# Retention and two gated layers on one core: pairs adjacent in memory, a decay table spread by a product, a mask made on the chip, work moved between engines, and rewritten order tables

## The chip, the cores and the metric

The kernel runs on one core of a Trainium2 chip. The metric is the device time of one execution in microseconds (us), median over runs. A core has TensorE (PE in the rows; PEld is its loading of weights), VectorE (DVE), ScalarE (ACT), GpSimd (POOL) and SyncE (SP, which only issues transfers here); 16 DMA engines move data between the chip's main memory and SBUF. PE writes to the eight banks of PSUM; DVE and ACT read and write PSUM and SBUF, and here POOL works on SBUF alone.

## What is computed

```python
gamma = 1.0 - 2.0 ** (-5.0 - np.arange(H))            # H = 8 heads, D = 64
for t in range(S):                                     # S = 768, batch 2
    state = gamma * state + outer(k[:, :, t], v[:, :, t])
    y[:, :, t] = (1 / sqrt(D)) * q[:, :, t] @ state
x = y.transpose(0, 2, 1, 3).reshape(1536, 512)
x = ((x @ w_a) * (x @ w_b)) @ w_out                    # d_ff 1536, first layer
h = x @ w_in                                           # d_ff 2048, second layer
out = (h * sigmoid(1.702 * h)) @ w_out2
```

q, k and v are float32; the five weight matrices arrive as 8-byte floats.

## The kernel before, in words

**Retention.** The 1536 tokens are 12 blocks of 128, six to a sequence (`SEQ`). For block n PE makes scores (`att_scores`, the "sc" products into `ps_sc`), adds the block's keys and values to a running state (`att_kv`, into `ps_kv`, which ACT copies to one of two `state` tiles), and makes the output from the masked scores (first half of `att_av`) and, but for a sequence's first block, from the state (second half, line 255), both into `ps_av`, of which there are three. Around it DVE multiplies the scores by the mask `causal` into `a` (line 207); `q` is multiplied by a decay table `qdec` and `v` by `vdec`, on POOL (lines 178 and 186, both recorded at helper line 75). Of `qdec`, `[P, SEQ, NP, P]`, one block's part is loaded and ACT makes the other five from it by a scale per partition (line 169). The four inputs of a block lie in memory as q, k transposed, k, v; the tile `qv` takes the first and the last, `kk` the two in between. Four buffers of each are there.

**Strassen sums and two parts.** The layers use products of halves (seven instead of eight, numbered 1 to 7 in `Job.step`), and each operand as a high part (a cast to float32r, on ACT) and a low part (source minus high part, `lo_part`, line 66), with three matmuls for each product. The rows of the first layer come from the retention: for each pair of blocks DVE forms sums (`att_x_vector`) and the tiles `a1h/a1l`, `s12h/s12l`, `s34h/s34l` and `a22` (shown as `a`). An `att_x_vector` chain and the low part of `s12` must be done before the block's `ps_av` bank can be written again.

**Weights.** A unit of weights is loaded into `wraw`, turned into float32 by ACT (`w_carry`) and DVE (`w_bits`, `w_sign`, `w_add`), summed (`w_sums`, four operations into `tt`) and split: `wd` for products 1 to 3, `wt` for the others (`w_hi` on ACT, `w_lo` on DVE). Units 0 to 11 are the first layer's jobs, 18 to 25 the second's.

**Order.** Each engine runs its instructions in the order in which the program emits them. In the retention the order inside a block is written out in the loop, with `BLOCK` telling which step of unit 0 or 1 goes where. `up` goes through products in the order `HEAD`, a loop, `TAIL`; after each, the table `UP` says how many steps of the weight stream (w) and of the postponed row work (l) are emitted. `down` does the same with `DOWN`, in "quarters" q of the output. A product 2 follows product 1 in the same PSUM pair `x`; products 6, 5, 3 follow each other in the pair `y`, into which ACT has copied `x` (line 722), and between them ACT copies `y` out (u2 after 6 at line 728, u4 after 5 at line 730). So product 3 cannot begin before the copy of u4 has read `y`. The very last quarter is done column group by column group:

```python
if last and q == 3:
    a = new_set("x")
    banks = [a[:, 0], a[:, 1], new_set("d")]
    for n in range(NG):
        for f in block:
            product(q, f, (n,), banks)
        flush(q, [(banks[n], n * G, (n + 1) * G)])
```

Before the first scores, and between the first blocks, PE runs 27 matmuls on zeros (`warm`).

Of the kernel before, what the change touches and what calls it, by code (L numbers as in the profile page):

```python
# [40 lines left out]
def retention_moe_kernel(  # L41
# [68 lines left out]

    causal = attp.tile([P, 1, P], F32, tag="causal", name="causal", bufs=1)
# [8 lines left out]
    qv_t, kk_t, q_t, v_t, a_t, x_t = {}, {}, {}, {}, {}, {}  # L120
# [3 lines left out]
    def att_load(n, part):  # L124
        if n >= NBLK:
            return
        if part == "qv":
            qv_t[n] = qv = attp.tile([P, 2, DM], F32, tag="qv", name="qv", bufs=RAWBUFS)
            if n > 0:
                nc.sync.dma_start(out=qv, in_=att[n][:, 0:4:3, :])  # L130
        else:
            kk_t[n] = kk = attp.tile([P, 2, DM], F32, tag="kk", name="kk", bufs=RAWBUFS)
            if n > 0:

                m = 1 if n % SEQ == SEQ - 1 else 2
                nc.sync.dma_start(out=kk[:, 0:m, :], in_=att[n][:, 1:1 + m, :])
        if n == 0 and part == "kk":
            qv = qv_t[n]
            nc.sync.dma_start(out=qv[:, 0, :], in_=att[n][:, 0, :])
            nc.scalar.dma_start(out=kk[:, 0, :], in_=att[n][:, 1, :])  # L140
            nc.scalar.dma_start(out=causal[:, 0, :], in_=cmask[:, 0:P])
            nc.scalar.dma_start(
                out=vdec[:, 0].rearrange("p h o -> p (h o)"), in_=cdec[:, NP * P:NP * P + H]
            )
            nc.sync.dma_start(out=qv[:, 1, :], in_=att[n][:, 3, :])
            nc.sync.dma_start(out=kk[:, 1, :], in_=att[n][:, 2, :])
            nc.scalar.dma_start(out=qdec[:, 1].rearrange("p a t -> p (a t)"), in_=cdec[:, 0:NP * P])
# [25 lines left out]
    def att_q(n):  # L173
        if n < NBLK:
            t = attp.tile([P, NP, P], F32, tag="q", name="q", bufs=3)
            q = qv_t[n][:, 0, :].rearrange("p (a t) -> p a t", t=P)
            for k in (slice(0, NP),) if n == 1 else (slice(0, 2), slice(2, NP)):
                mul(nc.vector if n == 1 else nc.gpsimd, t[:, k], q[:, k], qdec[:, n % SEQ, k])
            q_t[n] = t

    def att_v(n):
        if n < NBLK:
            t = attp.tile([P, H, D], F32, tag="v", name="v", bufs=3)
            v = qv_t[n][:, 1, :].rearrange("p (h d) -> p h d", d=D)
            for k in (slice(0, NP), slice(NP, H)):
                mul(nc.gpsimd, t[:, k], v[:, k], vdec[:, n % SEQ, k].to_broadcast([P, NP, D]))
            v_t[n] = t

    def att_scores(n):
# [4 lines left out]
        q = qv_t[n][:, 0, :].rearrange("p (a t) -> p a t", t=P) if n == 0 else q_t[n]  # L194
        for p in range(NP):
            for h2 in range(2):
# [3 lines left out]
                    kk_t[n][rows, 0, p * P:(p + 1) * P],  # L200
# [14 lines left out]
    def att_kv(n):  # L215
# [7 lines left out]
        for p in range(NP):  # L223
            for h2 in range(2):
# [3 lines left out]
                    kk_t[n][:, 1, h * D:(h + 1) * D],  # L228
# [108 lines left out]
    def att_s_lo(n):  # L337
        if n > 0 and n % 2 == 1:
            hi, lo = s_parts(n, 0)
            lo_part(nc.vector, lo, halves(av_t.pop(n)), hi)  # L340
            t, right = x_t.pop(n - 1), x_t.pop(n)
# [5 lines left out]
            later.append(lambda: [lo_part(nc.vector, lo, src, hi) for (hi, lo), src in parts])  # L347
# [17 lines left out]
    units = [*units_of(1), *units_of(2)]  # L365
    wraw, wt, wtt = {}, {}, {}
# [114 lines left out]
    def d_operand(f, part):  # L481
# [6 lines left out]
        (0, 1): (('load', 0),),  # L488
        (1, 0): (('load', 1),),
        (1, 1): (('load', 2),),  # L490
        (2, 2): (('load', 3),),
        (3, 1): (('load', 0),),
        (4, 1): (('carry', 0), ('bits', 0)),
        (5, 0): (('sign', 0),),
        (6, 0): (('d', 0), ('load', 1)),
        (7, 1): (('add', 0), ('later', 0)),
        (8, 1): (('load', 2),),
        (9, 0): (('load', 3),),
        (9, 2): (('carry', 1),),
        (10, 0): (('later', 0), ('bits', 1)),  # L500
        (11, 2): (('load', None), ('sums', 0)),
# [3 lines left out]
        (1, 2): ('', 'lll'),  # L505
        (1, 3): ('', 'ww'),
# [590 lines left out]
```

## Time and profile before

| | us |
|---|---|
| median of 3 runs | 589.77 (589.14 to 589.82) |
| the profiled execution's own time | 590.43 |
| its span in the trace | 588.60 |
| PE busy in the span | 572.1 |
| retention ends, first product of the first layer starts | 55.8 |
| DVE busy in the span | 418.8 |

Times in the trace count from the start of the span; 1.83 us of the profiled execution's own time lie around it. PE is busy for 97% of the span, but busy is not the same as needed: the warm-up matmuls count too, and a stretch with waits is found only when PE's idle time is read stage by stage.

### The profile page before, as it was taken

Reading aid. Unit: us, or ns where it says so; the run is one execution under the profiler, and the core shown is the slowest. Engines: PE = TensorE matmul, PEld = TensorE weight load, DVE = VectorE, ACT = ScalarE, POOL = GpSimd, SP = SyncE. Lnnn points to the kernel's source line nnn. Section 1 sums busy time; section 2 is a strip of 40 time slices with the busy share of each in tenths; the row PEclk is TensorE's granted clock in tenths of the full one; section 3 lists DMA queues with packets and bytes.
Section 4 is the critical chain, followed back from the end, with each engine's and each line's share of the span. In section 5 each row is a group of like instructions: output and inputs, shape, how many; then the busy total and the mean of one; then the engine's idle time right before and its main releaser. Section 6 shows DMA issues by size and latency. Waiting matters only on the chain.

```text
span 588.6 us, 8444 instructions
## 1 busy us (share of the span) xinstructions
PE 572.1 (97%) x3448; PEld 523.9 (89%) x3448; DVE 418.8 (71%) x478; ACT 296.2 (50%) x366; POOL 69.2 (12%) x145
## 2 busy tenths in 40 slices
PE   8978999999999999999999999999999999999996
PEld 8877999999999999888888889999998888888885
DVE  3789989788969788925788798766668636677322
ACT  3676654456545446535243578666667745160100
POOL 7783002021212111200000000000000000000000
PEclk9999999999999999999999999999999999999999
DMA  8992224433342221533422013665521635340022
GB/s 298 352 340 75 72 71 179 134 137 124 105 146 72 72 84 60 232 126 107 144 69 74 1 45 129 217 218 180 178 81 64 232 126 185 119 161 1 0 109 107
DMA packets 24583, 76.90 MB, mean 131 GB/s; under 512 B 2400, under 2 KB 2528, under 8 KB 24544
## 3 DMA queue, kind: packets, MB, share of 16 engines
q1 hardware_dynamic: 23968, 75.77, 37.2%
q10 hardware_dynamic: 576, 0.59, 0.4%
q8 instruction: 27, 0.44, 0.3%
q14 instruction: 12, 0.10, 0.1%
HBM read 60.62 MB, written 15.73 MB: 130 GB/s over the span
## 4 chain that ended last, share of the span: by engine, by line
PE 85%; DVE 9%; DMA 3%; ACT 1%; issue 1%; POOL 0%; ACTq 0%; DVEq 0%
PE ps L679 45%; PE ps L923 38%; DMA kk<-in_att_dram 2%; DVE a L207 1%; DVE s12l L66 1%; DVE sum L69 1%; DMA causal<-in_cmask_dram 1%; DVE sum L72 1%; DVE s34l L66 1%; PE ps_sc L198 1%; DVE a L66 1%; DVE x L69 1%; PE ps_av L244 0%; DVE wt L433 0%; DVE wt L66 0%
## 5 line engine op out<-in xcount | busy, mean ns | idle before, releaser
L923 PE MATMUL ps<-wt,ghl 128*128 128x512 f32 x576 | 131.1, 389 | 0.8 <-DVE sum L72 0.8
L923 PEld LDWEIGHTS ps<-wt,ghl 128*128 128x128 f32 x576 | 108.0, 188 | 23.6 <-DVE sum L72 1.2
L923 PE MATMUL ps<-ghl,wt 128*128 128x512 f32 x432 | 98.1, 389 | 0.0
L923 PEld LDWEIGHTS ps<-ghl,wt 128*128 128x128 f32 x432 | 81.1, 188 | 16.8
L679 PE MATMUL ps<-s12h,wt 128*128 128x384 f32 x320 | 87.2, 335 | 1.4 <-ACT ps L722 0.9
L679 PE MATMUL ps<-a1h,wd 128*128 128x384 f32 x320 | 87.4, 335 | 0.7 <-ACT ps L722 0.7
L66 DVE TENSOR_TENSOR ghl<-g,ghl 128x1536 fp32r<-128x1536 f32 x28 | 49.5, 1767 | 47.5 <-ACT ghl L272 47.5
L272 ACT CAST ghl<-g 128x1536 fp32r<-128x1536 f32 x28 | 40.9, 1482 | 56.2 <-PE ps L923 41.4
L72 DVE TENSOR_TENSOR sum<-ps,sum 128x512 f32<-128x512 f32 (+1 forms) x41 | 36.9, 932 | 39.0 <-PE ps L923 39.0
L679 PEld LDWEIGHTS ps<-s12h,wt 128*128 128x128 f32 x320 | 58.2, 188 | 2.1 <-ACT ps L722 1.2
L679 PEld LDWEIGHTS ps<-a1h,wd 128*128 128x128 f32 x320 | 58.3, 188 | 1.4 <-ACT ps L722 1.0
L679 PE MATMUL ps<-s12l,wt 128*128 128x384 f32 x160 | 53.7, 336 | 0.4 <-DVE s12l L66 0.3
L679 PE MATMUL ps<-a1l,wd 128*128 128x384 f32 x160 | 53.5, 334 | 0.0
L75 POOL TENSOR_TENSOR g<-g,u 128x768 f32<-128x768 f32 x12 | 30.0, 2500 | 162.5 <-DVE u L72 111.6
L433 DVE CUSTOM_DVE_ANT_0 wt<-wraw,wt 128x2048 uint16<-128x2048 uint16 x34 | 45.4, 1334 | 2.0
L679 PE MATMUL ps<-s34h,wd 128*128 128x384 f32 x160 | 44.2, 336 | 2.7 <-ACT u L730 2.7
L72 DVE TENSOR_TENSOR u<-ps,u 128x768 f32<-128x768 f32 x28 | 26.8, 955 | 27.3 <-PE ps L679 25.8
L679 PE MATMUL ps<-a,wt 128*128 128x384 f32 x240 | 44.8, 334 | 0.0
L679 PE MATMUL ps<-s34h,wt 128*128 128x384 f32 x160 | 43.8, 334 | 0.0
L679 PEld LDWEIGHTS ps<-a,wt 128*128 128x128 f32 x240 | 41.9, 188 | 0.0
L427 DVE SCALAR_TENSOR_TENSOR wt<-wraw,wt 128x1024 int32<-128x1024 int32 x34 | 41.4, 1218 | 0.4
L414 ACT ACTIVATE wt<-wraw 128x1024 f32<-128x1024 f32 x34 | 38.9, 1145 | 2.7 <-DMA kk<-in_att_dram 2.7
(92 smaller groups left out, 811.1 us busy)
## 6 DMA issues: line engine op xcount, KB each, us to landing
wraw<-in_w_dram SPq DMA_DIRECT2D x64, 512.0 KB, 4.5
spilled<-g SPq DMA_DIRECT2D x16, 768.0 KB, 7.4
g<-spilled SPq DMA_DIRECT2D x16, 768.0 KB, 6.0
qv<-in_att_dram SPq DMA_DIRECT2D x11, 512.0 KB, 7.1
kk<-in_att_dram SPq DMA_DIRECT2D x9, 512.0 KB, 7.1
wraw<-in_w_dram SPq DMA_DIRECT2D x8, 256.0 KB, 7.5
out_dram<-sum SPq DMA_DIRECT2D x3, 512.0 KB, 2.8
out_dram<-sum SPq DMA_DIRECT2D x6, 256.0 KB, 2.4
```

What stands on the lines that cost most here:

```text
L66: engine.tensor_tensor(out=lo, in0=src, in1=hi.bitcast(F32), op=ALU.subtract)
L69: nc.vector.tensor_tensor(out=o, in0=a, in1=b, op=ALU.subtract)
L72: nc.vector.tensor_tensor(out=o, in0=a, in1=b, op=ALU.add)
L75: engine.tensor_tensor(out=o, in0=a, in1=b, op=ALU.mult)
L198: nc.tensor.matmul(ps[:, h2, p * P:(p + 1) * P], kk_t[n][rows, 0, p * P:(p + 1) * P], q[rows, p, :], start=(p == 0), stop=True, skip_group ...
L207: nc.vector.tensor_tensor(out=a, in0=ps.rearrange("p c (a t) -> p (c a) t", t=P), in1=causal.to_broadcast([P, 2 * NP, P]), op=ALU.mult,)
L272: nc.scalar.copy(hi, src)
L414: nc.scalar.activation(out=wt[i], in_=high.bitcast(F32), func=ACTF.Abs)
L427: nc.vector.scalar_tensor_tensor(out=ti, in0=wraw[i][:, :, 1], scalar=-0x40000000, in1=ti, op0=ALU.bitwise_and, op1=ALU.bitwise_or)
L433: nc.vector.tensor_tensor(out=ti, in0=ti, in1=wraw.pop(i)[:, :, 0], op=ALU.add)
L679: nc.tensor.matmul(ps[b][:, 0] if len(ps) > 1 else ps[0][:, b], w_operand(self.key, i, wp)[:, kc * P:(kc + 1) * P], r.operand(i, xp)[:, kc ...
L923: nc.tensor.matmul(banks[n], l, r, start=(f == block[0] and i == 0), stop=(f == block[-1] and i == 2), skip_group_check=True,)
```

## The change

1. A block's inputs are taken as two adjacent pairs, `qk` (q and transposed k) and `vk` (k and v), each with one transfer; all loads go through SP, those of blocks 0 and 1 first. The layout in main memory is as it was.
2. The table of q's decay for one block is no longer loaded (256 KB). Two rows of it are, into a zeroed tile `pair`, and one PE product (`att_qdec_first`) spreads them over 128 partitions; ACT copies the result to `qdec`. Of the constants for its other parts, three of five are made by POOL products instead of memsets.
3. The mask is a memset and an `affine_select` on POOL, in place of a 64 KB load and a DVE comparison.
4. `ELSEWHERE`: ACT scales some heads of v (23 heads in nine blocks); q of blocks 3 and 4 goes to DVE; in the layers POOL makes the sums of seven units, six `wt` and five `wd` low parts (DVE before), and DVE makes six of the twelve gate products that POOL made.
5. `ORDER`, `BLOCK`, `UP`, `DOWN`, `HEAD` and `TAIL` are rewritten. 16 of the 27 warm-up matmuls go.
6. The last quarter of the second layer puts each column group in a PSUM bank of its own.
7. Buffers of the rows are counted free when the low part is emitted and no earlier (`row_done`); `att_s_lo` is cut in two.

The core of the diff:

```diff
+    def att_qdec_first():
+        ps = ps_att.tile([P, NP, P], F32, tag="av", name="ps_qdec", bufs=3).rearrange("p a t -> p (a t)")
+        nc.tensor.matmul(
+            ps, pair[:, NP * P:NP * P + P], pair[:, 0:NP * P], start=True, stop=True, skip_group_check=True
+        )
+        nc.scalar.copy(qdec[:, 1].rearrange("p a t -> p (a t)"), ps)
...
-            for k in (slice(0, NP), slice(NP, H)):
-                mul(nc.gpsimd, t[:, k], v[:, k], vdec[:, n % SEQ, k].to_broadcast([P, NP, D]))
+            heads = H - ELSEWHERE.get(("v", n), 0)
+            for k in (slice(0, NP), slice(NP, heads)) if heads > NP else (slice(0, heads),):
+                mul(nc.gpsimd, t[:, k], v[:, k], vdec[:, n % SEQ, k].to_broadcast([P, k.stop - k.start, D]))
+            for h in range(heads, H):
+                nc.scalar.activation(
+                    out=t[:, h], in_=v[:, h], func=ACTF.Copy, scale=vdec[:, n % SEQ, h]
+                )
...
-        lo_part(nc.gpsimd if key in POOL_LO.get(kind, ()) else nc.vector, t[:, 1, 0:n], src, t[:, 0, 0:n])
+        on_pool = ELSEWHERE.get((kind, units.index(("j", *key))), 0) if len(key) == 3 and key in job_keys else 0
+        lo_part(nc.gpsimd if on_pool else nc.vector, t[:, 1, 0:n], src, t[:, 0, 0:n])
...
     TAIL = {
-        1: ((-1, 7), (0, 1), (-1, 3), (0, 2), (0, 6), (-1, 4), (0, 7), (0, 5), (0, 3), (0, 4)),
-        2: ((0, 1), (-1, 7), (-1, 3), (0, 2), (0, 6), (-1, 4), (0, 5), (0, 7), (0, 3), (0, 4)),
+        1: ((0, 1), (-1, 7), (0, 2), (0, 6), (0, 7), (0, 5), (-1, 3), (-1, 4), (0, 3), (0, 4)),
+        2: ((0, 1), (-1, 7), (0, 2), (0, 6), (-1, 3), (0, 7), (0, 5), (-1, 4), (0, 3), (0, 4)),
     }
...
                 if last and q == 3:
-                    a = new_set("x")
-                    banks = [a[:, 0], a[:, 1], new_set("d")]
+                    banks = [new_set("d") for _ in range(NG)]
```

In `TAIL` an entry is (job, product), job 0 being the stage's last and -1 the one before it. In the first stage, first half of this table, PE's rows show what lies between product 5 and product 3 of the last job; `ps` with its number is the PSUM tile, `s12`, `s34` and `a22` are row operands, `wt` and `wd` weights. Before, the end of product 5 (into `ps_2231`) and the start of product 3 (into the same tile):

```order
702 L679 MATMUL ps_2231<-s12h_428,wt_2094 128x384 x2
703 L679 MATMUL ps_2231<-s12l_429,wt_2094 128x384
704 L679 MATMUL ps_2231<-s12h_428,wt_2094 128x384
705 L679 MATMUL ps_2231<-s34h_451,wd_2072 128x384
706 L679 MATMUL ps_2231<-s34l_452,wd_2072 128x384
707 L679 MATMUL ps_2231<-s34h_451,wd_2072 128x384 x2
```

The same place in the changed program, from the end of product 5 (into `ps_2190`) to the start of product 3:

```order
692 L992 MATMUL ps_2190<-s12h_404,wt_2124 128x384
693 L992 MATMUL ps_2070<-s34h_428,wd_1998 128x384
694 L992 MATMUL ps_2070<-s34l_429,wd_1998 128x384
695 L992 MATMUL ps_2070<-s34h_428,wd_1998 128x384 x2
696 L992 MATMUL ps_2070<-s34l_429,wd_1998 128x384
697 L992 MATMUL ps_2070<-s34h_428,wd_1998 128x384 x2
698 L992 MATMUL ps_2070<-s34l_429,wd_1998 128x384
699 L992 MATMUL ps_2070<-s34h_428,wd_1998 128x384 x2
700 L992 MATMUL ps_2070<-s34l_429,wd_1998 128x384
701 L992 MATMUL ps_2070<-s34h_428,wd_1998 128x384
702 L992 MATMUL ps_2208<-a22_430,wt_2020 128x384 x12
703 L992 MATMUL ps_2190<-s34h_428,wd_2088 128x384
```

Products 3 and 4 of the job before, 24 matmuls into other tiles, now stand between the two.

On PE at the start of the program (`ps_warm` the warm-up, `ps_sc` scores, `ps_kv` keys and values, `ps_av` output), before:

```order
1 L965 MATMUL ps_warm<-state_82 128x128 x11
2 L198 MATMUL ps_sc<-qv,kk 128x128 x8
3 L965 MATMUL ps_warm<-state_82 128x128 x8
4 L226 MATMUL ps_kv<-v,kk 64x64 x8
5 L244 MATMUL ps_av<-a,v 64x128 x8
6 L965 MATMUL ps_warm<-state_82 128x128 x3
7 L198 MATMUL ps_sc<-q,kk 128x128 x8
8 L965 MATMUL ps_warm<-state_82 128x128 x5
9 L198 MATMUL ps_sc<-q,kk 128x128 x8
```

and in the changed program:

```order
1 L1291 MATMUL ps_warm<-state_82 128x128 x11
2 L275 MATMUL ps_sc<-qk 128x128 x8
3 L195 MATMUL ps_qdec<-pair 128x512
4 L303 MATMUL ps_kv<-v,vk 64x64 x8
5 L275 MATMUL ps_sc<-q,qk 128x128 x8
6 L321 MATMUL ps_av<-a,v 64x128 x16
7 L332 MATMUL ps_av<-q,state_83 64x128 x8
8 L303 MATMUL ps_kv<-v,vk 64x64 x8
9 L275 MATMUL ps_sc<-q,qk 128x128 x16
```

The warm-ups after the first scores are gone, the product that spreads the decay table stands third, and the scores of block 2 (now in row 9, before in row 9 too) come behind block 1's output and state, which stood behind them.

On PE in the last quarter of the second layer (the last quarter's twelve matmuls for each of three column groups), before:

```order
1741 L923 MATMUL ps_4764<-wt_4615,ghl_4493 128x512 x3
1742 L923 MATMUL ps_4764<-wt_4615,ghl_4603 128x512 x3
1743 L923 MATMUL ps_4764<-wt_4488,ghl_4459 128x512 x3
1744 L923 MATMUL ps_4764<-wt_4488,ghl_4474 128x512 x3
1745 L923 MATMUL ps_4764<-wt_4615,ghl_4493 128x512 x3
1746 L923 MATMUL ps_4764<-wt_4615,ghl_4603 128x512 x3
1747 L923 MATMUL ps_4765<-wt_4488,ghl_4459 128x512 x3
```

and in the changed program:

```order
1739 L1242 MATMUL ps_4751<-wt_4602,ghl_4474 128x512 x3
1740 L1242 MATMUL ps_4751<-wt_4602,ghl_4590 128x512 x3
1741 L1242 MATMUL ps_4752<-wt_4500,ghl_4443 128x512 x3
1742 L1242 MATMUL ps_4752<-wt_4500,ghl_4459 128x512 x3
1743 L1242 MATMUL ps_4752<-wt_4602,ghl_4474 128x512 x3
1744 L1242 MATMUL ps_4752<-wt_4602,ghl_4590 128x512 x3
1745 L1242 MATMUL ps_4753<-wt_4500,ghl_4443 128x512 x3
```

Column groups 0 and 1 shared the tile `ps_4764`; now each group has its own.

## Rows read from the trace of the kernel before

**Rows 1.** The page: busy time, share of the span, instructions.

```profile
PE 572.1 (97%) x3448; PEld 523.9 (89%) x3448; DVE 418.8 (71%) x478; ACT 296.2 (50%) x366; POOL 69.2 (12%) x145
```

**Rows 2.** What PE waited for from 56 us on: total, times, longest.

```profile
PE ps L679 <- ACT u L730: 2.7, 3, 1.4
PE ps L679 <- ACT ps L722: 1.6, 2, 0.9
PE ps L923 <- DVE sum L72: 0.8, 1, 0.8
...
```

**Rows 3.** Timeline of PE, three matmuls: start, length, in brackets the wait.

```profile
230.56 0.44 PE L679 MATMUL ps<-s34h,wd 128*128 128x384 f32 x1 [0.94 <-ACT u L730]
...
353.02 0.45 PE L679 MATMUL ps<-s34h,wd 128*128 128x384 f32 x1 [0.34 <-ACT u L730]
...
448.80 0.45 PE L679 MATMUL ps<-s34h,wd 128*128 128x384 f32 x1 [1.43 <-ACT u L730]
```

**Rows 4.** The chain that ended last, in order of time: start, length, what.

```profile
13.97 1.16 PE ps_sc L198 x16
...
60.81 1.23 DVE wt L66
...
235.00 92.54 PE ps L923 x408
...
453.23 125.18 PE ps L923 x552
```

**Rows 5.** Busy time by stretch up to 62.03 us; last: clock, DMA share, GB/s.

```profile
0.00:7.10 7.10, 5.64 (x40) 5.40 (x41) 1.20 (x4) 0.00 (x0) 4.94 (x80) 1.00 0.70 192
7.10:14.00 6.90, 6.63 (x82) 5.89 (x80) 3.14 (x3) 4.04 (x10) 4.80 (x12) 1.00 1.02 395
14.00:24.40 10.40, 9.95 (x186) 9.19 (x188) 7.32 (x11) 8.88 (x26) 8.83 (x17) 1.00 1.02 375
24.40:32.20 7.80, 7.05 (x124) 6.22 (x118) 4.10 (x8) 3.66 (x7) 5.68 (x9) 1.00 1.00 343
32.20:62.03 29.83, 24.90 (x364) 21.81 (x364) 29.37 (x47) 21.66 (x46) 14.93 (x18) 1.00 0.50 167
```

**Rows 6.** Timeline of the first 6 us: the zeroing, the first warm-ups.

```profile
0.92 1.02 DVE L971 MEMSET state<- 128x512 f32 x2 [0.92 <-PEq L1087]
...
1.46 4.32 PE L965 MATMUL ps_warm<-state 128*128 128x128 f32 x22 [1.46 <-DVE state L971]
```

**Rows 7.** Groups by line and shape: count, busy us, mean ns, idle before.

```profile
L75 POOL TENSOR_TENSOR g<-g,u 128x768 f32<-128x768 f32 x12 | 30.0, 2500 | 162.5 <-DVE u L72 111.6 <-issue 50.8
...
L66 DVE TENSOR_TENSOR wt<-tt,wt 128x1024 fp32r<-128x1024 f32 x20 | 28.7, 1435 | 4.0 <-ACT wt L446 4.0
...
L66 DVE TENSOR_TENSOR wd<-wt,wd 128x768 fp32r<-128x768 f32 x20 | 19.1, 952 | 3.3 <-ACT wd L446 3.3
L75 POOL TENSOR_TENSOR v<-qv,vdec 128x256 f32<-128x256 f32 x24 | 17.8, 765 | 1.1 <-DMA qv<-in_att_dram 1.0
...
L69 DVE TENSOR_TENSOR tt<-wt 128x256 f32<-128x256 f32 x40 | 15.1, 420 | 0.4
...
L169 ACT ACTIVATE qdec<-qdec,early 128x128 f32<-128x128 f32 x20 | 6.2, 389 | 0.1
...
L75 DVE TENSOR_TENSOR q<-qv,qdec 128x512 f32<-128x512 f32 x1 | 0.7, 693 | 1.8 <-DMA qv<-in_att_dram 1.8
```

**Rows 8.** Busy time by stretch: the first layer's products without a wait.

```profile
75.40:229.60 154.20, 154.18 (x888) 153.88 (x888) 125.21 (x143) 79.25 (x89) 24.00 (x10) 1.00 0.33 113
```

**Rows 9.** Timeline of 180 to 196 us: a POOL product, two DVE additions.

```profile
180.83 2.70 POOL L75 TENSOR_TENSOR g<-g,u 128x768 f32<-128x768 f32 x1 [3.73 <-issue]
...
181.96 2.65 DVE L433 CUSTOM_DVE_ANT_0 wt<-wraw,wt 128x2048 uint16<-128x2048 uint16 x1
...
195.17 1.21 DVE L433 CUSTOM_DVE_ANT_0 wt<-wraw,wt 128x2048 uint16<-128x2048 uint16 x1
```

**Rows 10.** Busy time by stretch: PE waits here for half of the time.

```profile
32.00:36.00 4.00, 1.78 (x32) 1.55 (x32) 3.97 (x5) 3.53 (x8) 4.00 (x4) 1.00 1.03 395
```

More of the change, by code (lines that the diff above doesn't have):

```diff
@@ L126, in att_load @@
             return
[L127 to L130, printed above, removed]
-        else:
[L132 to L147, printed above, removed]
+        t = attp.tile([P, 2, DM], F32, tag=part, name=part, bufs=RAWBUFS)
@@ new lines, in att_load, with att_first @@
+        (qk_t if part == "qk" else kv_in)[n] = t
+        i = 0 if part == "qk" else 2
+        if part == "vk" and n % SEQ == SEQ - 1:
+            nc.sync.dma_start(out=t[:, 1, :], in_=att[n][:, 3, :])
+        else:
+            nc.sync.dma_start(out=t, in_=att[n][:, i:i + 2, :])
+    pair = rawp.tile([P, 2 * DM], F32, tag="wt", name="pair", bufs=2)
+    def att_first():
+        att_load(0, "qk")
+        nc.scalar.dma_start(out=pair[0:P:64, 0:NP * P], in_=cdec[0:P:64, 0:NP * P])
+        nc.scalar.dma_start(
+            out=vdec[:, 0].rearrange("p h o -> p (h o)"), in_=cdec[:, NP * P:NP * P + H]
+        )
+        att_load(0, "vk")
+        att_load(1, "qk")
+        att_load(1, "vk")
@@ L149, in att_constants @@
+    def att_qdec_first():
+        made.add(1)
+        ps = ps_att.tile([P, NP, P], F32, tag="av", name="ps_qdec", bufs=3).rearrange("p a t -> p (a t)")
[3 more added lines that the diff above has]
+        nc.scalar.copy(qdec[:, 1].rearrange("p a t -> p (a t)"), ps)
+    made = set()
     def att_constants():
         gamma = [1.0 - 2.0 ** (-5.0 - h) for h in range(H)]
+        nc.vector.memset(pair[:, 0:NP * P + P], 0.0)
+        for h2 in range(2):
+            nc.vector.memset(pair[64 * h2:64 * h2 + 1, NP * P + 64 * h2:NP * P + 64 * h2 + 64], 1.0)
+        nc.gpsimd.memset(causal, 1.0)
+        nc.gpsimd.affine_select(
+            out=causal[:, 0, :],
+            in_=causal[:, 0, :],
+            pattern=[[1, P]],
+            compare_op=ALU.is_ge,
+            fill=0.0,
+            base=0,
+            channel_multiplier=-1,
+        )
@@ L158, in att_constants @@
                 nc.gpsimd.memset(gdec[rows, c, h // 2:h // 2 + 1], gamma[h] ** (float(P) * (c - 1)))
+        for c in range(3, SEQ):
+            nc.gpsimd.tensor_tensor(out=gdec[:, c], in0=gdec[:, c - 1], in1=gdec[:, 2], op=ALU.mult)
     def att_vdec(cs):
@@ L165, in att_qdec @@
     def att_qdec(c):
+        assert 1 in made
+        made.add(c)
         if c < SEQ and c != 1:
@@ L365, in retention_moe_kernel @@
     units = [*units_of(1), *units_of(2)]
+    job_keys = {u[1:] for u in units if u[0] == "j"}
     wraw, wt, wtt = {}, {}, {}
@@ L487, in retention_moe_kernel @@
     BLOCK = {
[L488 to L491, printed above, removed]
-        (3, 1): (('load', 0),),
[L493 to L501, printed above, removed]
+        (-1, 2): (('load', 0),),
@@ L611, in at_block @@
             "carry": w_carry, "bits": w_bits, "sign": w_sign, "add": w_add, "d": w_direct_whole,
-            "sums": w_sums, "load": w_dma, "later": lambda _: later.pop(0)(),
+            "sums": w_sums, "load": w_dma, "qdec": att_qdec,
+            "later": lambda _: later.pop(0)[1](),
         }
         for step, i in BLOCK.get((n, place), ()):
+            after = dict(bits="carry", sign="bits", add="sign", d="add", sums="add").get(step)
+            assert after is None or (steps[after], i) in begun, (step, i)
             begun.add((steps[step], i))
@@ L674, in products @@
             r = rows_of[self.ph]
-            finish(("row", {1: 1, 2: 1, 4: 4, 5: 5, 6: 5, 7: 7, 3: 7}[i]))
+            row = {1: 1, 2: 1, 4: 4, 5: 5, 6: 5, 7: 7, 3: 7}[i]
+            assert not any(row in rows for rows, _ in later), (self.key, i)
+            finish(("row", row))
             for b in range(2):
@@ L771, in g_load @@
     def g_load(f):
+        whole.add(f)
         chunk[f] = t = row_tile("g")
@@ L839, in tick @@
             g_next(ph, fb * FB + 2 * FB)
+            if load_at[ph] < (C1, C2)[ph - 1] and room["row"] <= max(4 - len(sums), 0):
+                finish()
             g_fetch(ph, max(4 - len(sums), 0))
```

462 lines of the change are left out of this document (370 added, 92 removed), and 13 rows, old and new, of the table ORDER.

## The prediction

> **What bounds the kernel now.** I read PE first, since it is busy for 97% of the span [rows 1]. Busy is no bound by itself, so I read which stretches hold a wait. The first layer's products run from 75.40 to 229.60 us with 154.18 us busy of 154.20 [rows 8]. Both output stages stand on the chain as single pieces of PE, 92.54 and 125.18 us long [rows 4]. In these 372 us no reordering can gain; it can only lose. What can be had lies before 75 us and in a few waits behind.
>
> Those behind are in the list of PE's waits: from 56 us on, 2.7 us in three waits for the copy of u4 (line 730), 1.6 us in two for the copy at line 722, and 0.8 us for DVE's sum at line 72 [rows 2]; the list's two other rows hold 0.8 us together. The three waits for u4 are 0.94, 0.34 and 1.43 us long [rows 3].
>
> For the retention I read the stretches [rows 5]. The reader is to see that the bound changes inside them. Up to 32.20 us the DMA engines are fully busy (share 1.00 to 1.02 from 7.10 on), DVE for half of the time. From 32.20 to 62.03 us DVE is busy for 29.37 of 29.83 us, and PE, idle for 4.9 us there, waits for it. The chain agrees: it leaves DVE for good with the low part of the first unit's weights, at 60.81 to 62.03 us [rows 4, 5]. So the retention is worth what DVE gains. Summed over rows 5, DVE has worked 45.1 us by 62.03 and been idle for 16.9, 16.4 of it before 32.20. Only that idle time can be won, by feeding DVE earlier.
>
> **The change, part by part.** *Loads, mask and decay table.* 320 KB less is loaded before the first scores. After 7.10 us 395 to 343 GB/s arrive [rows 5]; 2 MB of weights and 12 MB of inputs at 360 GB/s take 39 us, and in the changed order the last inputs are asked for by block 11, near 45 us. I take loading as no bound of the changed retention, so the 16.4 us of DVE idle are no longer set by DMA but by the start-up chain. That chain I work out.
>
> PE's warm-up begins when DVE has zeroed the state, 1.02 us for 1024 columns [rows 6]. Now DVE first zeroes 640 columns of `pair` and writes two short rows: 640/1024 of 1.02 is 0.64, with the rows 0.8 us. Warm-up and first scores move back by that, the scores' end to about 7.7 us. Next on PE stands the product for the decay table: by the warm-up (22 rows of 128 columns, two for each matmul, in 4.32 us [rows 6]) a 512-column matmul costs up to 1.6 us; the stretch after the warm-up runs faster, so I take 1.2 (bounds 0.6 and 1.6). ACT then does one copy, eight scales, two heads of v, four scales and two state copies, 17 operations of 0.31 us (6.2 us for 20 [rows 7]; bound 0.39 each): 5.3 us. At 14.2 us block 1's state is there, and its state product, 0.9, and keys and values, 0.6, end at 15.7. The scores of block 2 now stand behind these, so they start at about 15.8 us, against 13.97 before [rows 4]. Those of block 3 follow at once, at 17.0. Before, a block's other products stood between: 64 rows a block at 9.95 us for 186 [rows 5] are 3.4 us, so block 3 began at 17.4. PE is only 0.4 us ahead by then; what changes is that nothing of unit 0 has to be waited for later.
>
> DVE, until then: idle 5.9 us before its first mask, as before [rows 5]. From about 9 us to the mask of block 2, at 17 us, it has two q's and one x of 0.69 us [rows 7] and one mask of 1.2, 3.3 of 8 us: 4.7 idle. From 17 us on its work outruns PE's (before it had 4.1 of 7.8 us to do from 24.40 to 32.20 [rows 5], since unit 0's weights came late). Two gaps I see later: about 1 us before the mask of block 5, where PE at 3.4 us a block is the slower, and about 0.9 where the output of block 8 needs the PSUM bank of block 5, whose low part now stands behind the addition and the first low part of unit 0: 1.9 us. Idle in all: 12.5 us. Work: 45.1, less 0.2 for the comparison (a quarter of q's 512 columns), plus 1.4 for two q's, plus 0.8 for the zeroing, 47.1. The low part ends at 59.6, not 62.03: **-2.4 us**. Bounds: all old idle time stays, 45.1 + 2.0 + 16.9 = 64.0, a loss of 2.0; or the later stalls and half of the start-up gap go, 47.1 + 8.3 = 55.4, a gain of 6.6, of which PE could use about 5 (its own idle time in that stretch [rows 5]).
>
> *v's heads on ACT* (23 of them, at most 0.39 us each, 9 us, spread over 35 us) and *q on DVE* are in this sum. ACT was busy for 21.7 of 29.8 us in the tight stretch [rows 5], so 9 us more would have filled it there; that is the price if the heads come late, and one reason why I keep a loss in the bounds.
>
> *The tails of the product stages.* Product 3 of the last job followed product 5 at once, and had to wait for the copy of u4. In the changed order two products (stage 1) or one (stage 2) stand between. A product of 12 matmuls takes 2.1 us (154.2/888 [rows 8] times 12); the waits were 0.94 and 1.43 us [rows 3]. They vanish: **-2.4 us** in sum. Bounds: if ACT's work ahead of the copy is later by as much as is gained, 0. The third wait, 0.34 us, and the two at line 722 stay: product 2 or 6 still follows product 1 directly there.
>
> *The last quarter.* Column group 1 waited 0.8 us for the sum of group 0 [rows 2], which reads the tile that group 1 writes. With a tile for each group nothing orders the two: **-0.8 us**. Bounds 0 (if the bank that is taken still waits for an older sum) and 0.8.
>
> *Work moved to POOL.* In the first layer's products POOL gets five `wd` parts (as wide as the gate product, 2.5 us each), six `wt` parts in all (1024/768 of that, 3.3; five of them here) and the sums of four units (four operations of 0.77 us, 3.1), and gives six gate products to DVE [rows 7]. POOL goes from 24.0 us [rows 8] to 24.0 - 15.0 + 12.5 + 16.7 + 12.3 = 50.5 of 154.2. DVE loses 5 x 0.95 + 5 x 1.44 + 4 x 1.7 and gains 6 x 0.95, so 13 us less of 125.2. DVE had no PE behind it there, so this gains nothing. What hides POOL's slowness is the lead of the weights: the program emits those low parts three to six products ahead of their use, at least 6.2 us, and a cast (0.9) with a `wd` part takes 3.4. If that cover is gone, each microsecond is PE's. I take 0, bounds 0 and +1 us for each of the ten.
>
> POOL also slows DVE. While POOL ran a gate product from 180.83, the addition at 181.96 took 2.65 us; the one at 195.17, with POOL idle, 1.21 [rows 9]. One POOL operation can cost DVE 1.4 us; 26 us more of POOL, at 2.5 us each, cost up to 15 us, which against 13 us saved leaves DVE with 27 of the 29 us that it had free [rows 8]. The sum stays. The Trainium skill, GPSIMD Engine Reference, 4.1 Engine selection, says that element-wise work belongs on VectorE, GpSimd being about twice as slow with two inputs, and 8 Key points that the two share their SBUF interfaces; by that alone moving these parts would be a loss, and the trace agrees with the second point (2.65 against 1.21 us).
>
> *Rewritten `UP`, `DOWN`, `BLOCK` and row counts.* They move ACT and DVE steps between products, in stretches where PE waits for nothing. They can only add; the trace of before shows what one misplaced step costs, 0.34 us [rows 3]. I take one such wait, **+0.3**.
>
> Sum: -2.4 - 2.4 - 0.8 + 0.3 = -5.3 us. The profiled execution took 590.43 us, 0.66 above the median of 589.77. From its own time the sum gives 585.1, from the median 584.5.
>
> **The rivals.** *The start-up gains nothing.* ACT's 17 operations stand in one queue between the table and block 1's state, and q of block 3 waits there too; if ACT or POOL (whose mask operation no row prices; a product of 256 columns there takes 0.77 us [rows 7]) is 2.5 us later than I say, DVE's idle time is as before. The tails remain: 589.8 - 2.9 = 586.9 us.
>
> *DVE is fed better than I think*, the gain being 5 us: 582.
>
> *Slower: POOL's low parts come late.* Eleven parts that DVE made in 0.95 or 1.44 us take 2.5 or 3.3, behind one another and behind the gate products. It decides from half a microsecond of PE wait for each part, since 11 x 0.5 is the whole gain. At 0.8 us each, 8.8 - 5.3: 593 us. For it: units 4 to 7 have both parts on POOL, 23 us of work in some 58. Against it: the lead of 6.2 us.
>
> *PE's clock.* The start has 16 warm-up matmuls fewer and gaps of some 5 us in all up to 16 us. In the rows PE was busy for 1.78 of 4.00 us, and the granted clock stayed at 1.00, the 2.4 GHz level [rows 10]; the start is busier than that. If it fell to 1.2 GHz there, the 8 us of PE work up to 16 us would take up to 8 more, half of it in gaps: +4, 588.5 us. The Trainium skill, TensorE: Matmul & The Clock Gate, What's actually happening, says that the clock is halved after PE has been idle; rows 10 show no fall at less than half busy.
>
> **How the numbers follow.** The forecast, 584.5 us, has a chance of 0.52; the better feeding 0.10; the start-up without gain 0.20; the clock 0.06; POOL late 0.12. The range from 581 to 590 leaves out the last and part of the second: the low end is the sum with 5 us from the retention and a little over, 589.8 - 5 - 3.2; the high end takes in a retention that loses 2 us, tails that gain half, and two more waits. This kernel's median can be told from no change at about 0.2%, 1.2 us. Faster by more than that, below 588.6: the first three, and nothing of the others, 0.82 with rounding down to 0.81. Within it: the clock and a mild loss from POOL, 0.08. Slower: 0.11.
>
> **What would show it.** Right: DVE's low part of the first `wt` ends near 59.6; scores of block 2 near 15.8 and of block 3 straight behind; no wait of PE for u4 at the two tails; no wait of PE for DVE in the last quarter; PE without a wait between about 73 and 227. Wrong: PE waiting for POOL's `wt` or `wd` in that stretch, a clock below 1.00 before 20 us, or DVE idle for more than 15 us up to its first `wt` part.

## The result, and the profile after

The changed kernel takes 583.92 us (median of 4 runs, 583.50 to 585.10); on the same chip the kernel before takes 589.45. The ratio is 0.9912, 95% interval 0.9892 to 0.9931: faster by 5.5 us, where 5.3 were forecast. The profiled execution took 584.11 us; its span is 582.4 us. One execution of run e8, further down, took 952 us at a mean granted clock of 0.559, for which nothing here gives a reason; without it e8's median is 586.13 and not 586.17.

The page's first line, which answers to [rows 1]:

```profile
PE 570.0 (98%) x3418; PEld 521.8 (90%) x3418; DVE 408.5 (70%) x449; ACT 302.0 (52%) x390; POOL 89.4 (15%) x153
```

PE's waits over the whole span (total, times, longest), for [rows 2]:

```profile
PE ps_warm L1291 <- DVE state L1298: 2.6, 1, 2.6
PE ps L992 <- ACT ps L1035: 1.3, 2, 0.9
PE ps L992 <- DVE wt L66: 1.1, 1, 1.1
PE ps_sc L275 <- issue: 0.9, 1, 0.9
...
```

No row names the copies of u4 (line 1043 now), and none the sum in the last quarter. The copy that was at line 722 (1035 now) is still waited for twice. No row of the layers names POOL.

The chain that ended last (start, length, what), for [rows 4]:

```profile
57.98 1.23 DVE wt L66
59.26 12.44 PE ps L992 x70
72.61 143.81 PE ps L992 x828
...
231.50 92.33 PE ps L1242 x406
...
447.84 130.72 PE ps L1242 x576
```

DVE's first low part of `wt` ends at 59.2 us, 2.8 earlier than in [rows 4]; on the chain the output stages start 3.5 and 5.4 us earlier. Read from the first product of each (the first one counted from the product at 59.26, behind the low part), the stages last 171.55, 98.29, 118.58 and 134.70 us (first layer up and down, second layer up and down, with the end); before, 172.76, 97.96, 120.27 and 135.58. So the retention gave 2.82 us, the stages 1.21, -0.33, 1.69 and 0.88: 6.27 in all, the difference of the spans. A second trace of the kernel before (run e12 below) has the same four stage lengths, but an end of the retention 0.9 earlier. The stages' lengths also repeat to 0.1 us in the eight later traces that leave `TAIL`, `UP`, `DOWN` and the banks as changed. So the 3.45 us of the stages are firm; the retention's share is not. By the medians it is 5.5 less 3.45, about 2.1 us.

Busy time by stretch (length, then PE, PEld, DVE, ACT, POOL; granted clock, DMA share, GB/s), for [rows 5], and the stretch that answers to [rows 8]:

```profile
0.00:7.10 7.10, 4.46 (x21) 4.46 (x22) 1.79 (x5) 1.28 (x1) 4.08 (x65) 1.00 0.69 234
7.10:14.00 6.90, 6.01 (x71) 4.22 (x71) 3.14 (x3) 3.88 (x13) 4.41 (x9) 1.00 1.02 384
14.00:24.40 10.40, 10.35 (x186) 9.39 (x188) 7.72 (x12) 9.72 (x31) 4.69 (x11) 1.00 0.89 310
24.40:32.20 7.80, 6.91 (x119) 6.25 (x116) 6.72 (x12) 7.70 (x18) 4.09 (x7) 1.00 1.01 383
32.20:59.20 27.00, 24.54 (x374) 21.96 (x369) 26.62 (x45) 21.70 (x50) 12.55 (x18) 1.00 0.48 178
...
72.60:226.80 154.20, 154.19 (x889) 154.19 (x890) 115.47 (x122) 78.59 (x88) 43.24 (x31) 1.00 0.30 106
```

The reader is to see DVE in the fourth row: busy for 6.72 us of 7.80, where it had 4.10 [rows 5]. The first three rows give it 1.0 us more than before, of which 0.9 is the zeroing of `pair`. So DVE's gain isn't at the start, but at 24 to 32 us. What stood there before is a row of DVE's timeline that the prediction didn't show, with ScalarE's pass that it waits for (in brackets the idle time ahead, and its end):

```profile
30.28 1.19 ACT L414 ACTIVATE wt<-wraw 128x1024 f32<-128x1024 f32 x1 [2.74 <-DMA kk<-in_att_dram]
31.50 0.69 DVE L420 TENSOR_SCALAR wt<-wt 128x1024 f32<-128x1024 f32 x1 [2.57 <-ACT wt L414]
```

That is the first step of unit 0 (`w_carry`, then `w_bits`), and the same pass in the changed kernel:

```profile
25.96 1.19 ACT L503 ACTIVATE wt<-wraw 128x1024 f32<-128x1024 f32 x1
```

SyncE issued the last quarter of unit 0's weights at 22.39 us before, and now as the last of three, from 20.18 to 20.61 (SP's timeline; the next load of weights, at 25.13 before, is the first quarter of unit 1):

```profile
22.39 0.42 SPq L402 DMA_DIRECT2D wraw<-in_w_dram  x1
```

```profile
19.24 1.37 SPq L490 DMA_DIRECT2D wraw<-in_w_dram  x3
```

That transfer took 7.8 us from issue to landing before and 5.7 now, so it landed at 30.2 and 25.9 us, each time just ahead of the pass. So the theory to test is that the retention's gain is unit 0's earlier arrival, for the last quarter a move of one entry in `BLOCK`, from (2, 2) to (2, 0). Its rival, the prediction's own account, is the start-up chain, made of tables, order, heads of v and pairs. For the rest the theory is the prediction's: the tails, the bank, nothing from POOL.

### The profile page after: what moved, and what is told of

Read it like the earlier page. It is cut to its first block, busy times and chain, and to the rows that moved or that the text cites. A ratio compares the mean times of both kernels' runs of the same rounds, so it can differ in the third digit from the quotient of the medians.

```text
span 582.4 us, 8412 instructions
## 1 busy us (share of the span) xinstructions
PE 570.0 (98%) x3418; PEld 521.8 (90%) x3418; DVE 408.5 (70%) x449; ACT 302.0 (52%) x390; POOL 89.4 (15%) x153
## 4 chain that ended last, share of the span: by engine, by line
PE 84%; DVE 11%; issue 1%; ACT 1%; DMA 1%; POOL 0%; ACTq 0%; DVEq 0%; POOLq 0%
PE ps L992 44%; PE ps L1242 38%; DMA vdec<-in_cdec_dram 1%; DVE ghl L66 1%; DVE s12l L66 1%; DVE a L284 1%; PE ps_sc L275 1%; DVE sum L69 1%; DVE s34l L66 1%; DVE sum L72 1%; PE ps_av L332 1%; DVE wt L66 1%; DVE wt L516 1%; DVE wt L522 1%; DVE a L66 1%
## 5 line engine op out<-in xcount | busy, mean ns | idle before, releaser
L66 DVE TENSOR_TENSOR ghl<-g,ghl 128x1536 fp32r<-128x1536 f32 x28 | 50.7, 1815 | 37.8 <-ACT ghl L349 37.8
L522 DVE CUSTOM_DVE_ANT_0 wt<-wraw,wt 128x2048 uint16<-128x2048 uint16 x34 | 41.5, 1221 | 1.8 <-DVE wt L516 0.5
L555 POOL TENSOR_TENSOR tt<-wt 128x256 f32<-128x256 f32 x14 | 10.1, 740 | 192.7 <-DVE wt L522 192.7
```

Of the source, the lines that this page charges most:

```text
L66: engine.tensor_tensor(out=lo, in0=src, in1=hi.bitcast(F32), op=ALU.subtract)
L522: nc.vector.tensor_tensor(out=ti, in0=ti, in1=wraw.pop(i)[:, :, 0], op=ALU.add)
L555: engine.tensor_tensor(out=tt[:, o], in0=a, in1=b, op=op)
```

## The experiments

Each kernel was timed beside the kernel before on one chip; times are medians. The kernel before itself came out at 589.00 to 589.56 us in the four series, so differences of half a microsecond between runs of different series say little. In the table "pass" is the start of ScalarE's first pass over unit 0, "low part" the end of the first low part of `wt`, both from the trace.

| | us | before, same chip | ratio, 95% | pass | low part |
|---|---|---|---|---|---|
| before, first trace | 589.77 | | | 30.28 | 62.03 |
| e12 before, second trace | 589.53 | 589.56 | | 28.94 | 61.11 |
| changed | 583.92 | 589.45 | 0.9892 to 0.9931 | 25.96 | 59.20 |
| e1 early start | 582.83 | 589.00 | 0.9886 to 0.9913 | 24.86 | 58.71 |
| e2 v, q on POOL | 583.80 | 589.00 | 0.9895 to 0.9922 | 24.25 | 57.69 |
| e3 tables loaded | 584.03 | 589.00 | 0.9903 to 0.9930 | 26.34 | 58.88 |
| e4 fixed order | 583.75 | 589.00 | 0.9898 to 0.9925 | 25.60 | 58.45 |
| e5 unit 0 late | 589.72 | 589.34 | 0.9999 to 1.0018 | 32.17 | 64.94 |
| e6 before, unit 0 early | 588.90 | 589.34 | 0.9986 to 1.0003 | 27.73 | 60.43 |
| e7 old tails, shared bank | 594.07 | 589.34 | 1.0069 to 1.0099 | 25.98 | 58.62 |
| e8 old `UP`, `DOWN` | 586.17 | 589.34 | 0.9929 to 0.9968 | 26.53 | 59.22 |
| e9 strided pairs | 584.44 | 589.56 | 0.9911 to 0.9937 | 26.65 | 60.72 |
| e10 layers' work on DVE | 583.68 | 589.56 | 0.9890 to 0.9920 | 25.67 | 58.73 |
| e11 e1 and e2 together | 582.32 | 589.56 | 0.9867 to 0.9895 | 24.99 | 57.87 |

**e1: the start first.** `state[0]` is zeroed ahead of `pair`, vdec goes ahead of `pair` on ScalarE's queue.

```diff
+        nc.vector.memset(state[0], 0.0)
         nc.vector.memset(pair[:, 0:NP * P + P], 0.0)
...
-        for t in state:
-            nc.vector.memset(t, 0.0)
+        nc.vector.memset(state[1], 0.0)
```

> DVE zeroes the tile that the warm-up reads before it zeroes `pair`, and the 4 KB transfer of vdec goes ahead of that of `pair`. Theory: the retention is paid by VectorE's idle time at the start (13.2 us up to the first low part, in the changed kernel), so that a start of the warm-up 1.0 us earlier ends the first low part 0.8 to 1.0 us earlier, near 58.3 instead of 59.20, and the time falls to about 583.0. Rival: the start is held by the chain of ScalarE behind the decay table and by GpSimd's v; then the scores of block 2 stay at 16.98 and the time at 583.9.

Measured 582.83; PE's warm-up starts 1.1 us earlier (its wait for `state` is 1.5 us, as before, not 2.6), the low part ends 0.5 earlier. It is 1.1 us below the changed kernel by the medians, 0.6 when each is taken from its own runs of before; the intervals overlap. The direction is the theory's, the size is open.

**e2: v and q back on GpSimd.**

```diff
-        ('q', 3): 1,
...
-        ('v', 1): 2,
...
-        ('v', 11): 2,
```

> All heads of v and q of blocks 3 and 4 go back to GpSimd. Theory: before the change nothing on PE or DVE waited for GpSimd, and GpSimd is busy for 29.8 of 59.2 us, so later blocks lose nothing; only blocks 1 to 3, where 10 heads (about 0.19 us each on GpSimd) and one q are due at once, come later, by 1 us at most: 584 to 585. Rival: moving this work is what feeds VectorE, and without it the whole gain of the retention, 2.8 us, goes: 586.7, with waits of PE for v and q of GpSimd of some 3 us.

Nothing was lost: 583.80. The low part ended 1.5 us earlier, in an execution that was itself 1.3 us faster than this median. The rival is wrong.

**e3: table and mask loaded.**

```diff
-        nc.scalar.dma_start(out=pair[0:P:64, 0:NP * P], in_=cdec[0:P:64, 0:NP * P])
+        nc.scalar.dma_start(out=causal[:, 0, :], in_=cmask[:, 0:P])
...
+        nc.scalar.dma_start(out=qdec[:, 1].rearrange("p a t -> p (a t)"), in_=cdec[:, 0:NP * P])
```

> The decay table and the mask are loaded as before (320 KB more, a comparison on DVE), without the spreading product and its zeroed tile; order and everything else as changed. Theory: loading isn't the bound of the retention, and the product takes the place of a transfer that would land at about the same time; 320 KB at 390 GB/s are 0.8 us, partly given back by the 0.8 us of zeroing that go: 584 to 584.8. Rival: the tables carry the gain of the retention; without them VectorE waits for the mask and for q as before, and the time is 586.7 with the first low part near 62.

584.03, low part at 58.88: the tables carry none of the gain.

**e4: one order for blocks 1 to 11.**

```diff
-        -1: (0, 'sc', 'v', 'av', 'kv', 'q', 'hi', 'lo', '34', 'sums', 'x', 2, 1),
+        -1: ('sc', 'hi', 0, 'q', 'v', 'kv', 'sums', 'lo', '34', 1, 'av', 'x', 2),
```

Rows 1 to 11 of `ORDER` go, but for the 2 ahead of 1 in block 7.

> Blocks 1 to 11 of the retention are emitted in one fixed order, that of the kernel before; block 0 keeps its new order, and the loads of unit 0 and the inputs stay. Theory: what the retention gained comes from the start-up chain (block 0) and from unit 0 being loaded early; the order inside later blocks is worth 1 us at most, so 584 to 585, first low part at 59.2 to 60.2. Rival: the written-out order carries the gain; first low part near 62, 586.7.

583.75: the order written out block by block carries none of it either.

**e5: unit 0 late in the changed kernel.**

```diff
-        (2, 0): (('load', 3),),
...
-        (3, 1): (('load', 0),),
+        (3, 2): (('load', 3), ('load', 0)),
```

> The changed kernel with the last quarter of unit 0's weights asked for behind the inputs of blocks 7 and 8, as in the kernel before (there issued at 25.13 us, in the changed kernel by 20.6). Theory, new after the trace of the changed kernel and the runs on the start: what the retention gained is the wait of DVE for unit 0 (2.57 us from 28.93 to 31.50 in the kernel before, ScalarE's first pass having waited 2.74 for the transfer). Then the first pass starts near 30 us instead of 25.96, DVE waits again, and the time rises by 1.5 to 2.8, to 585.4 to 586.7. Rival: the start-up chain made the gain; no change, 583.9.

589.72: the whole gain of the change is gone, and more than the theory gave. ScalarE's timeline, the pass:

```profile
32.17 1.12 ACT L503 ACTIVATE wt<-wraw 128x1024 f32<-128x1024 f32 x1 [6.25 <-DMA qk<-in_att_dram]
```

The pass came 6.2 us later and the low part 5.7. The expectation took the 25.13 us of the kernel before for this quarter; it is unit 1's. The quarter was issued at 22.39 there and at 23.66 here, behind one more block's inputs, and the pass starts 1.9 and 3.2 us later than in the two traces of before. So the edit goes beyond a return to the old place. The price is larger for two more reasons. ScalarE, standing at the pass, now also holds heads of v, and PE waited 3.6 us for them; and behind that wait PE's granted clock fell to 0.50 (last section). The run shows that the changed kernel can't do with a late arrival. It doesn't show how much of the gain the early one made.

**e6: unit 0 early in the kernel before.**

```diff
-        (1, 0): (('load', 1),),
-        (1, 1): (('load', 2),),
-        (2, 2): (('load', 3),),
+        (1, 0): (('load', 1), ('load', 2)),
+        (1, 1): (('load', 3),),
```

> The kernel before with two of the four transfers of unit 0 asked for earlier, one by some 6 us and the last by two blocks, some 5 us; nothing else. Theory: DVE's wait of 2.57 us goes, and the time falls by 1.8 to 2.6, to 586.4 to 587.2, unless the inputs of blocks 7 and 8, which now come 0.7 us later, make PE wait. Rival: the start-up chain made the gain, and this edit does nothing: 589.0.

Only 0.4 us, within the uncertainty. (The last quarter was issued at 19.50 us, 2.9 and not 5 us earlier, for the same reason as in e5.) The low part ended 1.6 us earlier than in the first trace of before, but 0.7 earlier than in the second (e12), where the pass was 1.3 us earlier and DVE waited 1.1 us for it rather than 2.57: the arrival differs between the two traces, and the prediction's rows came from the later one. In e6 the wait for the pass is gone, and another has grown in its place. DVE's waits up to 62 us, of e6 and then of e12:

```profile
DVE a L207 <- PE ps_sc L198: 7.4, 6, 2.3
```

```profile
DVE a L207 <- PE ps_sc L198: 5.6, 5, 1.9
...
DVE wt L420 <- ACT wt L414: 1.1, 1, 1.1
```

DVE now waits 1.8 us longer for scores. The early arrival alone is not enough in the old order.

**e7: the old tails and the shared bank.** `TAIL` and the two lines on `banks` as before.

> The changed kernel with the tails and the shared bank of the last quarter of the kernel before; the two places are told apart in the trace. Theory of the prediction: waits of 0.94 (stage 1) and 1.43 us (stage 2) for the copy of u4 come back, and 0.8 us in the last quarter: 583.9 + 3.2 = 587.1. Rival: the wait of stage 2 went because the rewritten `UP` keeps other work of ScalarE away from the copy (before, product 7 stood between products 5 and 3 there too, and the wait of 1.43 us came from two passes of `w_carry` ahead of the copy); then only 0.9 and 0.8 come back: 585.6.

594.07, outside both. PE's timeline at the two tails, then ScalarE's queue ahead of the first:

```profile
230.59 0.69 PE L992 MATMUL ps<-s34h,wd 128*128 128x384 f32 x1 [4.38 <-ACT u L1043]
...
452.42 0.44 PE L992 MATMUL ps<-s34h,wd 128*128 128x384 f32 x1 [1.43 <-ACT u L1043]
...
226.77 1.04 ACT L535 CAST wt<-wt 128x1024 fp32r<-128x1024 f32 x1 [4.53 <-DVE wt L522]
227.72 1.13 ACT L503 ACTIVATE wt<-wraw 128x1024 f32<-128x1024 f32 x1
228.76 1.09 ACT L504 ACTIVATE wraw<-wraw 128x1024 int32<-128x1024 uint32 x1
229.75 0.78 ACT L1043 COPY u<-ps 128x768 f32<-128x768 f32 x1
```

In stage 2 the wait is back to the hundredth, with the new `UP`. So the new tail is what removed it, and the rival (that it was `UP`) is wrong. In stage 1 it is 4.38, not 0.94: the steps of `UP` go by a product's place in the order, so with another tail the copy of u4 falls behind a cast that waits for DVE. PE's clock fell behind this wait (below); the next 24 matmuls took 7.1 us instead of 4.2. Stage by stage against the changed kernel: 7.5 (4.4 and 2.9 of it named), 0.4, 1.7 and 1.0 us. The last holds the 0.8 us for the sum, which is back among PE's waits.

**e8: `UP` and `DOWN` as before.**

> The changed kernel with `UP` and `DOWN` of the kernel before; the tails are the new ones. Theory of the prediction: these tables are worth nothing, since PE waits for nothing around them, and the tails alone remove the waits: 583.9 to 584.3 (0.34 us for the third wait for u4). Rival, as in the run with the old tails: the wait in stage 2 is ScalarE's, and comes back with the old tables by up to 1.4 us: 585.3.

586.17: 2.2 us more than the changed kernel, more than either; its interval and the changed kernel's just overlap. PE's waits:

```profile
PE ps L795 <- ACT ps L838: 1.4, 2, 0.9
PE ps L795 <- DVE wt L66: 1.0, 1, 1.0
...
PE ps L795 <- ACT g L813: 0.4, 1, 0.4
PE ps L795 <- ACT u L846: 0.3, 1, 0.3
...
PE ps L795 <- DVE s12l L66: 0.3, 1, 0.3
```

The two tails' waits don't come back. The third for u4 does, and so does one for `s12l`; both were there before, 0.34 and 0.3. One for `g` is new. Stages: 172.20, 97.96, 119.28, 135.57 us. So beside the other edits the tables are worth 0.7 us in each of the `up` stages and 0.9 in the last, less 0.3 in the first `down`. The last 0.9 comes at two places near the start of that stage. At 465.90 PE waits for a copy of `sum`. At 456.51 its weight load waits for a low part of `ghl`, which on DVE stands behind two steps of the weight stream:

```profile
453.38 0.69 DVE L509 TENSOR_SCALAR wt<-wt 128x1024 f32<-128x1024 f32 x1
454.10 0.69 DVE L510 TENSOR_SCALAR wt<-wt 128x1024 int32<-128x1024 int32 x1
454.71 1.75 DVE L66 TENSOR_TENSOR ghl<-g,ghl 128x1536 fp32r<-128x1536 f32 x1
...
456.51 0.53 PEld L1045 LDWEIGHTS ps<-wt,ghl 128*128 128x128 f32 x3 [0.54 <-DVE ghl L66]
```

The kernel before, with these same tables, loses time at neither place. So this 0.9 is what the other edits would cost with the old tables, and no gain over the kernel before.

**e9: the pairs as before.**

```diff
-            nc.sync.dma_start(out=t, in_=att[n][:, i:i + 2, :])
+            nc.sync.dma_start(out=t, in_=att[n][:, 0:4:3, :])
```

k is then read from the other tile, and block 0's four parts come one by one.

> The changed kernel with the inputs paired as before: q and v in one tile with a strided transfer, transposed k and k in the other; block 0's four parts come one by one in the order q, transposed k, k, v. Everything else as changed. Theory: the pairs matter for when a buffer comes free and so for when SP gets to the last quarter of unit 0's weights; a tile that holds v is kept longer than one with q and transposed k, so the weights come later by 0 to 2 us, and since their arrival sets the retention's end, the time rises by as much: 584 to 586. Rival: the pairing does nothing, 583.9.

584.44, half a microsecond more, within the uncertainty. Unit 0's arrival is nearly unchanged; its trace has a fall of the clock at the start.

**e10: the layers' work back on DVE.** All entries `d`, `t`, `sums` and `mul` of `ELSEWHERE` go.

> The changed kernel with the work of the layers put back: sums and low parts of the weights on DVE, the six gate products on GpSimd; order tables as changed. Theory of the prediction: DVE has no PE behind it in the first layer's products, so this changes nothing, 583.9 within 0.6. Rival: the rewritten tables were made for a DVE that is relieved, and without that its low parts come late: PE waits for `wt` or `wd` of DVE, slower by over 1.5, 585.5 or more.

583.68, no wait of PE for a low part behind the first (0.7 us at the retention's end), and in the stretch that answers to the row above:

```profile
72.60:226.80 154.20, 154.20 (x891) 154.20 (x891) 121.37 (x141) 79.15 (x89) 25.22 (x11) 1.00 0.30 106
```

18 us of GpSimd's work relieve DVE by 6 us, and nobody waits for either.

**e11: e1 and e2 together.**

> The early start (first run) with all of v and q back on GpSimd (second run). Theory: each microsecond by which the start or the arrival of unit 0 is earlier ends the retention earlier; the early start gave 1.1 us against the changed kernel, and the second run's retention ended 1.5 us earlier in its trace while its time was only 0.1 lower: 582.0 to 582.8. Rival: they don't add, 583.

582.32, ratio 0.9881: the fastest of all, 1.6 us below the changed kernel by the medians; the intervals just overlap.

**e12: a second trace of the kernel before.**

> The kernel before once more, for a second trace: the one that the prediction read has a span 1.2 us above the usual one of 587.4. Theory: the retention's end moves with the arrival of unit 0's weights from run to run, so the missing microsecond is there: the first low part ends near 61 instead of 62.03, DVE's wait for ScalarE's first pass being shorter by as much, and the real gain of the retention is then about 1.8 and not 2.8 us. Rival: the microsecond lies in the layers, and the low part ends near 62 again.

The low part ended at 61.11, DVE's wait for the pass was 1.1: as expected.

## Why the prediction was right, and which of its steps were not

**The retention, -2.4.** The size holds: -2.8 between the two traces, about -2.1 by the medians, and four traces with the changed retention (the changed kernel, e7, e8, e10) end it at 58.6 to 59.2 against 61.1 and 62.0 before. The account of DVE holds roughly: 46.0 us of work and 13.2 of idle time up to 59.2, where 47.1 and 12.5 were forecast. But the step "the 16.4 us of DVE idle are no longer set by DMA but by the start-up chain" failed as a cause. The start-up chain came later than worked out: the state was zeroed 1.2 us later rather than 0.8, the warm-up took 5.06 us rather than 4.32, DVE was idle for 7.2 us before its first mask rather than 5.9, and the scores of block 2 began at 16.98, not at 15.8 (those of block 3 did follow at once). So that the size came out is luck: the chain which the sum works out ran over a microsecond late, and the idle time that went lies elsewhere. Where most of it lay is in half a sentence there, "since unit 0's weights came late": DVE's wait for the pass, 2.57 us before, is gone. e5 puts off loads of weights alone and loses 5.8 us, while undoing heads of v, tables, order or pairs one by one cost 0.5 us at most. In all 14 traces the low part ends 31.8 to 34.1 us after ScalarE's first pass over unit 0; the two go together, but that spread of 2.3 us is nearly as large as the gain. So the early arrival is needed (e5, at a price that holds more than the arrival), but it doesn't make the gain alone: in the old kernel DVE then waits for scores instead (e6). What made the gain is therefore not shown, and which of the other edits has to go with the arrival stays open. Heads of v, tables, the order of blocks 1 to 11 and the pairs, undone singly, were not needed; the new order of block 0, the later places of `bits` and `sign` in `BLOCK`, the missing warm-ups and the loads that all go through SP were not tried by themselves.

**The tails, -2.4.** Both waits went, and e7 shows that the tail removes them. But "product 3 of the last job followed product 5 at once" was true of stage 1 alone. In stage 2 product 7 stood between them before as well, and what was late was the copy of u4 itself, behind a cast and two passes of `w_carry` in ScalarE's queue. In the new order the copy goes first (it starts at 441.64 us, the cast at 445.46): a place in ScalarE's queue, not in PE's.

**The last quarter, -0.8.** Right: the wait is gone, the stage is 0.9 shorter, and with the shared bank the wait of 0.8 is back (e7). e8, with a bank for each group, has no such wait either.

**The tables, +0.3.** Wrong in sign. "They can only add" overlooked the two waits of 0.34 and 0.3 us that the prediction itself had counted. The stages gave 3.45 us, of which the waits at the two tails and in the last quarter are 3.15. So 0.3 us of gain is left for the tables, where the sum took a loss of 0.3. e8 puts the tables at about -2 us, but beside the other edits: of what it loses, only those two waits stood in the kernel before.

**POOL, 0.** Right (e10). GpSimd was busy for 43.2 us in the stretch, not 50.5: `wt` took 2.48 us, not 3.3, and `wd` 1.90, not 2.5. The rival of late low parts didn't come.

**The clock.** It stayed at 1.00 in the changed kernel up to 59 us. The rival is real all the same, as the last section shows.

## What to carry to other kernels

Ask for each wait which transfer ends it and where that transfer stands in its queue, before crediting the compute chain ahead of it: here asking for the last quarter of a unit's weights 3.5 us later cost 5.8 us, PE's wait and the clock behind it included, while tables, order and pairings could each be undone at 0.5 us or nothing. When a wait is for a copy, read the queue of the engine that copies: the product order on PE may look clear while a cast stands ahead of the copy. And read two traces of the kernel before: a term read from one stall of 2.57 us was 1.1 in the second trace.

## What the runs showed of the hardware

**The clock fell behind three gaps of PE, and not behind every gap of such a length.** In e7 PE was idle for 4.38 us up to 230.59. Stretches of its trace, with the granted clock third from the end:

```profile
225.00:227.00 2.00, 1.21 (x7) 0.89 (x6) 1.68 (x2) 0.23 (x1) 0.00 (x0) 1.00 0.00 0
227.00:230.50 3.50, 0.00 (x0) 0.00 (x0) 1.23 (x1) 3.50 (x5) 0.00 (x0) 0.92 0.69 249
230.50:234.00 3.50, 3.41 (x11) 3.41 (x12) 0.96 (x1) 2.79 (x3) 1.84 (x1) 0.50 0.14 55
234.00:236.00 2.00, 2.00 (x8) 2.00 (x7) 1.17 (x2) 0.00 (x0) 0.00 (x0) 0.50 0.00 0
236.00:238.00 2.00, 2.00 (x11) 1.96 (x10) 2.00 (x2) 0.00 (x0) 0.00 (x0) 0.80 0.00 0
```

0.50 is the 1.2 GHz level; it stood there while PE was busy again, and products 3 and 4 paid for it. In e9 PE was idle for 1.87 us up to 10.82 and busy again when the same fall came:

```profile
12.00:13.00 1.00, 1.00 (x16) 0.91 (x14) 0.00 (x0) 1.00 (x5) 1.00 (x3) 0.76 1.07 406
13.00:14.00 1.00, 1.00 (x10) 0.87 (x10) 0.76 (x1) 1.00 (x4) 1.00 (x3) 0.50 1.02 399
14.00:15.00 1.00, 1.00 (x14) 1.00 (x12) 0.47 (x1) 0.39 (x2) 1.00 (x5) 0.50 1.02 391
15.00:16.00 1.00, 1.00 (x14) 1.00 (x12) 0.78 (x2) 0.05 (x1) 0.95 (x3) 0.54 1.05 391
```

In e5 it was the wait for heads of v, 3.61 us up to 34.60, with the clock's row behind it:

```profile
34.60 1.19 PE L321 MATMUL ps_av<-a,v 128*64 128x128 f32 x7 [3.61 <-ACT v L261]
...
36.00:38.00 2.00, 2.00 (x27) 2.00 (x25) 1.97 (x4) 2.00 (x6) 0.00 (x0) 0.50 0.64 223
```

[Rows 10] hold waits of 1.45 and 1.65 us, PE less than half busy, and no fall. Nor did one follow in e9 itself behind a later gap, which was longer than the one at 10.82:

```profile
50.63 0.69 PE L308 MATMUL ps_kv<-v,vk 128*64 128x64 f32 x16 [2.21 <-ACT state L318]
...
50.00:52.00 2.00, 1.37 (x33) 1.40 (x35) 1.91 (x4) 1.90 (x7) 0.00 (x0) 1.00 0.00 0
52.00:54.00 2.00, 2.00 (x42) 2.00 (x40) 1.93 (x5) 1.06 (x3) 0.00 (x0) 1.00 0.04 8
```

So the length of a gap alone doesn't decide between these two. The changed kernel's largest wait behind its first product is 1.1 us.

**A small transfer beside large ones.** vdec, 4 KB, took 6.59 us from issue to landing in the changed kernel, beside 512 KB loads, with 343 GB/s arriving in that time; GpSimd waited 3.9 us for it. No run here has it alone. Making the mask on GpSimd took 0.2 us for the memset and 0.3 for the `affine_select` of 128 by 128, which no row of before had priced.
